# Heads paired with the next but one, joined loads of later batches and a reordered w_in, in a fused sliding-window attention and leaky-ReLU MLP kernel

## The chip, the cores and the metric

The kernel runs on one core of one Trainium2 chip. The metric is the time of one execution on the device in microseconds, taken as the median over several runs. A core has five engines that run on their own instruction streams, each in program order: TensorE (PE, with its weight loads shown as PEld), VectorE (DVE), ScalarE (ACT), GpSimd (POOL) and SyncE (SP). Here SP does nothing but issue transfers (DMAs), which sixteen DMA engines carry out.

## The reference

Attention with a mask for each head, then a two-layer MLP over all tokens:

```python
B, H, S, D = 8, 8, 576, 64           # q, k, v: (B, H, S, D), float32
scores = q @ k^T / sqrt(D)
rel = pos[:, None] - pos[None, :]
mask_plain = (rel >= 0) & (rel < 32)                        # heads 0 to 3
mask_dil = (rel >= 0) & (rel < 128) & (rel % 4 == 0)        # heads 4 to 7
attn = softmax(where(mask, scores, -1e9))
x = (attn @ v).transpose(0, 2, 1, 3).reshape(B * S, H * D)  # 4608 x 512
h = x @ w_in                                                # w_in: 512 x 2048
out = maximum(0.01 * h, h) @ w_out                          # w_out: 2048 x 512
```

## The kernel before

All of w_in and w_out is held in SBUF as 16-bit floats. The batches of attention are worked in order, and two batches make 1152 tokens of x^T in `xt`, with 128 of the 512 rows of x^T in each of four blocks. These are the outputs of a pair of heads, 64 rows for each. The MLP takes the tokens in chunks of 384: `up` (L983) makes hidden columns by four products over the four blocks of `xt` and the four 128-row parts of w_in, ScalarE applies the leaky ReLU into `gt`, and `down` and `group` multiply by w_out. `group` takes four tiles of 128 tokens at a time and saves one product in eight with sums of blocks.

Nothing of the order is left to the hardware. Every operation is a task with a cost in microseconds, a priority and dependencies. `_Plan.run` (L97) lays the tasks out on the engines in a planned time, and each engine's instructions are then issued in the order of those planned starts. So a planner's cost changes the order, never the work. A transfer's planned cost has an issue on SP (0.42 for all, in `load`, L265), a service on one server for all DMAs (`took`, L258) and a margin `LATE`. `WHEN` (L17) holds the planned start of each batch.

Four heads make a group. Within a batch the group of dilated heads comes first, then the plain one (`attend`: pairs 2, 3, 0, 1). A pair is two heads that stand side by side, 0 and 1, 2 and 3 and so on; one head has partitions 0 to 63, the other 64 to 127.

`load_group` (L350) loads a group. Batch 0 and 1 are "early" and loaded in a form of their own. For batches 2 to 7 q and k each come as eight transfers, for each pair `j` one for every 32 partitions `a`, of 18 runs of 32 numbers on each partition:

```python
lo = [[load("SP", at(st, 32 * a, 32 * a + 32, j * S, [32, 18], [1, 32]),
            dram(src, base + (2 * j + a // 2) * HS + (a % 2) * 32,
                 [D, 32], [32 * D, 18], [1, 32]),
            576, 128, s_old, prio) for a in range(4)] for j in range(2)]
```

They land in staging buffers `stg` (four of them for late groups, one for q or k of a group), are cast by POOL into `nat` (three buffers, one for a pair), turned by VectorE and POOL into `slots`, and multiplied on TensorE in `late_unit` (L902): scores, Exp on ScalarE, a mask multiply on VectorE (`ee`, L952), sums and values, and a division into `xt` (L971). Plain v of a late group comes in four transfers of 64 x 9 x 64 numbers, dilated v in six smaller ones. All loads go on SP's queue; a load waits for its staging buffer to be free, and holds up what stands behind it on SP.

`load_rest` (L453) loads the last 64 rows of q and k of the early batches as 8 heads x 16 x 256 numbers. `load_w` (L484) loads the weights, w_in in eight transfers of 128 rows x 1024 columns (0.5 MB each):

```python
src = dram(moe_w_in, n % 4 * 128 * DFF + x, [DFF, 128], [1, 1024])
```

Transfers 0 to 3 hold the first 1024 columns of the four row parts, and 4 to 7 the others. `FIRST` (L20) orders the loads of the start: in it `i` is a w_in transfer, `o` a w_out transfer, and the others are q, k and v of the first two batches. `store` (L1034) writes results from three output tiles `osb`, on SP's queue as well.

Of the kernel before, what the change touches and what calls it, by code (L numbers as in the profile page):

```python
# [12 lines left out]
ALU = mybir.AluOpType  # L13

WIN = 32
AHEAD, LATE = 5.0, 4.0
WHEN = (-5.0, 15.0, 50.0, 77.0, 112.0, 138.0, 172.0, 200.0)  # L17
CON = -1484.5
AFTER = -1495.0
# [38 lines left out]

class _Task:
    __slots__ = ("choices", "eng", "lat", "deps", "fn", "prio", "soft", "n", "start", "done",  # L60
                 "dur", "left", "ready", "users", "service", "kind", "late")

    def __init__(self, choices, lat, deps, fn, prio, soft, n, kind):
        self.choices, self.lat, self.fn = choices, lat, fn
        self.prio, self.soft, self.n, self.kind = prio, soft, n, kind
        self.deps = [d for d in deps if d is not None]
        self.eng = self.start = self.done = self.dur = None
        self.left = 0
        self.ready = 0.0
        self.users = []  # L70
        self.service = self.late = 0.0


class _Plan:
# [22 lines left out]
    def run(self):  # L97
        free, waiting = {}, {}
        server = 0.0

        def enter(t):
            for eng, _ in t.choices:
                waiting.setdefault(eng, []).append(t)

        for t in self.tasks:
            for d in t.deps:
                d.users.append(t)
            t.left = len(t.deps)
            if t.left == 0:
                enter(t)  # L110
        order = []
        while len(order) < len(self.tasks):
            best = None
            for eng, cand in waiting.items():
                if not cand:
                    continue
                here = free.get(eng, 0.0)
                if eng == "SP":
                    here = max(here, server - AHEAD)
                could = [t for t in cand  # L120
                         if not self.better_elsewhere(t, eng, max(here, t.ready), free)]
                if not could:
                    continue
                at = max(here, min(t.ready for t in could))
                pick = min(((t.ready + t.soft > at + 1e-9, t.prio, t.n), t)
                           for t in could if t.ready <= at + 1e-9)
                if best is None or (at, pick[1].n) < best[:2]:
                    best = (at, pick[1].n, eng, pick[1])
            at, _, eng, t = best
            for e, _ in t.choices:  # L130
                waiting[e].remove(t)
            t.eng, t.start, t.dur = eng, at, dict(t.choices)[eng]
            free[eng] = at + t.dur
            if t.service:
                begin = max(at + t.dur + 0.9, server)
                server = begin + t.service
                t.done = server + 1.1 + t.late
            else:
                t.done = at + t.dur + t.lat
            order.append(t)  # L140
            for u in t.users:
                u.ready = max(u.ready, t.done)
                u.left -= 1
                if u.left == 0:
                    enter(u)
        order.sort(key=lambda t: (t.start, t.n))
        return order
# [3 lines left out]
def kernel(  # L151
# [112 lines left out]

    def load(queue, dst, src, n, size, deps, prio, slow=1.0):  # L265
        eng = ENG[queue]
        return plan.dma(queue, 0.42, took(n, size) * slow, deps,
                        lambda e: eng.dma_start(dst, src), prio,  # L268
                        LATE if prio > -1500 + len(FIRST) else 0.8 if prio >= AFTER else 0.0)

# [79 lines left out]
    def load_group(b, g, prio, prio_v):  # L350
# [7 lines left out]
        for o, src in ((0, q), (1, k)):  # L358
            sn, s_old = stage_slot(early, s_users := [])
            st = stg[sn]  # L360
            if first:
                lo = [load("SP", at(st, 0, 128, j * 512, [256, 2], [1, 256]),
                           dram(src, base + 2 * j * HS, [4 * D, 128], [HS, 2], [1, 256]),
                           256, 1024, s_old, prio + 0.3 * j + 0.1 * o) for j in range(2)]
            elif early:
                lo = [load("SP", at(st, 0, 128, 0, [256, 4], [1, 256]),
                           dram(src, base, [4 * D, 128], [HS, 4], [1, 256]),
                           512, 1024, s_old, prio)]
            else:
                lo = [[load("SP", at(st, 32 * a, 32 * a + 32, j * S, [32, 18], [1, 32]),  # L370
                            dram(src, base + (2 * j + a // 2) * HS + (a % 2) * 32,
                                 [D, 32], [32 * D, 18], [1, 32]),
                            576, 128, s_old, prio) for a in range(4)] for j in range(2)]
            stage.append((st, s_users))
            loads.append(lo)

# [4 lines left out]
                       dram(v, base, [4 * D, 128], [HS, 4], [1, 256]), 512, 1024, v_old, prio_v)]  # L381
            v_late[b] = vs, v_old, v_users
        elif dil:
            lv = [[load("SP", at(vs, 64 * h, 64 * h + 64, j * S, [256, 2], [1, 256]),
                        dram(v, base + (2 * j + h) * HS, [4 * D, 64], [256 * D, 2], [1, 256]),
                        128, 1024, v_old, prio_v) for j in range(2)] + [
                   load("SP", at(vs, 64 * h, 64 * h + 64, 512, [S, 2], [1, D]),
                        dram(v, base + h * HS + 512 * D, [D, 64], [2 * HS, 2], [1, D]),
                        128, 256, v_old, prio_v)] for h in range(2)]
        elif early:  # L390
            lv = []
# [7 lines left out]
                                96, 256, v_old, prio_v), t_vz]  # L399
                lv.append(lj)  # L400
        else:
            lv = [[load("SP", at(vs, 64 * h, 64 * h + 64, j * S, [D, 9], [1, D]),
                        dram(v, base + (2 * j + h) * HS, [D, 64], [64 * D, 9], [1, D]),
                        576, 256, v_old, prio_v) for j in range(2)] for h in range(2)]

        if not early:
            kn, k_old = ring("VK", NK, k_users := [])
# [11 lines left out]
        for j in range(2):  # L419
            nn, n_old = ring("NAT", NNAT, n_users := [])  # L420
            na, c_qk = nat[nn], []
            for o in range(2):
                st, s_users = stage[o]
                if early:
                    dst = at(na, 0, 128, o * 512, [D, 2], [128, 4], [1, D])
                    src = at(st, 0, 128, j * 512, [256, 2], [D, 4], [1, D])
                    n = 512
                else:
                    dst, src, n = na[:, o * S:o * S + S], st[:, j * S:j * S + S], S
                c_qk.append(cast(dst, src, n, (loads[o][j:j + 1] if first else loads[o] if early else loads[o][j]) + n_old, prio,  # L430
                                 (("ACT",) if o else ("DVE",)) if first and dil and j == 0 else
                                 CENG if early else ("POOL",)))
                s_users.append(c_qk[-1])
            if not early:
# [3 lines left out]
            dn, d_old = ring("VD" if dil else "VP", NV, d_users := [])  # L438
            vt = (vd if dil else vp)[dn]
            n_v = 256 if dil else 384  # L440
            h_a, h_s = 2 * j * n_v, n_v
            n, w = n_v // D, 128 * (8 if dil else 6)
            c_v = [cast(at(vt, 0, 128, 0, [w, 2], [128, n], [1, D]),
                        at(vs, 0, 128, h_a, [h_s, 2], [D, n], [1, D]), 2 * n_v,
                        (lv if dil else lv[j]) + d_old, prio_v)]
            v_users += c_v
            seen_ones[b, 2 * g + j] = [t_ones["d" if dil else "p", dn]]
            kept[b, 2 * g + j] = vt, d_users
# [4 lines left out]
    def load_rest(b, prio):  # L453
# [18 lines left out]
        for vi in (2, 3, 0, 1):  # L472
            vt, d_users = kept[b, vi]
            c_v = []
            if vi >= 2:
                c_v = [cast(at(vt, 0, 64, 0, [1024, 2], [128, 4], [1, D]),
                            at(vs, 0, 64, 1024 + (vi - 2) * 512, [256, 2], [D, 4], [1, D]), 512,
                            [lv] + d_users, prio + 30)]
                v_users += c_v
            visits[b, vi, 1] = rest, [c], r_users, vt, c_v + seen_ones[b, vi], d_users  # L480
# [3 lines left out]
    def load_w(n, prio):  # L484
# [5 lines left out]
        old = w_used[prev] if prev is not None else []  # L490
        if n < 8:
            x = n // 4 * 1024
            src = dram(moe_w_in, n % 4 * 128 * DFF + x, [DFF, 128], [1, 1024])
            dst, x = w_in, n % 4 * DFF + x
        else:
            x = 1024 * (n - 8)
            src = dram(moe_w_out, 128 * x, [2 * DM, 128], [1, 1024])
            dst = w_out
# [85 lines left out]
    def turn(b, hp, part, prio):  # L584
# [90 lines left out]
        if part == 1:  # L675
# [9 lines left out]
                new = pair_moves[b, hp ^ 1]  # L685
            else:
                new, busy = [], users + other[1] * (two == 2)
                for hh, h in enumerate(heads_of(b, hp)):
                    p0 = 64 * hh
                    for o, bk in ((0, qb), (1, kb)):  # L690
                        x, dims = 512 * o + 16 * h, [[128, 4], [1, 16]]
                        if dil:
# [3 lines left out]
                        else:  # L696
                            c, to = hh * S + 488, [[24, 4], [1, 16]]
                        step = PAD + S if o else 2 * S
                        new.append(move(at(bk, p0, p0 + 64, c, [step, two], *to),
                                        at(tpb, p0, p0 + 64, x, [32, two], *dims), 64 * two,  # L700
                                        [tq] + zq + zk + (busy if dil and o else []), prio))
                pair_moves[b, hp] = new
            q_users += new
# [330 lines left out]
    def store(ob, i, c, tt, c0, n_o, t_c, users, both=False):  # L1034
        for n_p, (p0, tok, n, by) in enumerate(rows(c, tt)):
            users.append(load("ACT" if both and n_p else "SP",
                              dram(out, tok * DM + c0, [by * DM, n], [1, n_o]),
                              ob[p0:p0 + n, i:i + n_o], n, 4 * n_o, [t_c], -3000))

    def down(c, tt, acts, at_time):  # L1040

# [359 lines left out]
```

## Time and profile before

| | |
|---|---|
| median of 3 runs | 354.02 us (350.91 to 355.02) |
| profiled execution, its own time | 354.57 us |
| span of its instructions | 352.8 us |
| TensorE busy | 309.0 us (88%), 2838 matmuls |
| VectorE, ScalarE, GpSimd busy | 206.5, 192.3, 128.5 us |
| granted TensorE clock, mean | 0.966 |
| transfers issued on SP | 421 |
| moved by DMA | 47.64 MB, 135 GB/s in the mean |

The span is that of the instructions in the profile; the execution's own time has 1.8 us more around it. The page has the span in 40 equal slices, with a digit for the busy tenths of each engine, and a list of idle times with the engine, line and tile that ended them (an arrow `<-` is read "waited for"). A `q` behind an engine's name (SPq) stands for its instruction queue: time in which it issues a transfer or waits, rather than computes. L268 is the line in `load` where every transfer is issued, and L278 the line of the casts, so that only the tile's name tells which is meant.

### The profile page before, as it was taken

The numbers are of one execution on the slowest core, as the hardware profiler recorded it, in microseconds if no ns is written. First come the engines' busy times: TensorE is split into PE (matmuls) and PEld (weight loads), VectorE is DVE, ScalarE is ACT, GpSimd is POOL, SyncE is SP. The second block draws the span as 40 slices with busy tenths as digits, with TensorE's granted clock in tenths as the row PEclk, the third lists the DMA queues.
The fourth block names the chain that finished last, engine by engine and source line by source line (L and its number), as shares of the span: only waits on it lengthen the run. The fifth ranks groups of instructions, "written<-read, shape, count | busy, mean of one in ns | idle before, by whom it ended". The sixth has DMA issues, their size and how long they took to land.

```text
span 352.8 us, 7717 instructions
## 1 busy us (share of the span) xinstructions
PE 309.0 (88%) x2838; PEld 221.8 (63%) x2838; DVE 206.5 (59%) x407; ACT 192.3 (55%) x465; POOL 128.5 (36%) x179
## 2 busy tenths in 40 slices
PE   8788898998789698859785987995999999999996
PEld 3534554678666576637563765764778777777775
DVE  5736997769748488424845873966462444015161
ACT  4835855877656475524680644643565584544422
POOL 3468555794553473246324644515000000000000
PEclk9999999999999899969996998998999999999999
DMA  7999989588679964576677768457300301021133
GB/s 252 294 335 372 390 228 161 129 141 150 139 133 141 122 138 95 122 129 143 119 153 129 142 131 142 128 111 151 94 17 14 91 0 32 0 91 32 30 92 89
DMA packets 159030, 47.64 MB, mean 135 GB/s; under 512 B 139024, under 2 KB 156304, under 8 KB 158992
## 3 DMA queue, kind: packets, MB, share of 16 engines
q1 hardware_dynamic: 158416, 46.79, 58.3%
q8 instruction: 22, 0.36, 0.4%
q10 hardware_dynamic: 576, 0.35, 0.4%
q14 instruction: 16, 0.13, 0.1%
HBM read 37.68 MB, written 9.44 MB: 134 GB/s over the span
## 4 chain that ended last, share of the span: by engine, by line
PE 35%; SPq 25%; DMA 21%; POOL 7%; DVE 5%; issue 4%; ACT 1%; POOLq 0%; DVEq 0%
SPq L268 25%; PE hps L999 16%; PE fps L1142 11%; DMA stg<-in_k_dram 7%; DMA stg<-in_q_dram 6%; PE tp L1142 3%; DMA wst<-in_moe_w_out_dram 3%; POOL nat L278 3%; DMA wst<-in_moe_w_in_dram 3%; DMA vst<-in_v_dram 3%; PE ops L942 2%; POOL slots L629 1%; POOL v_all L278 1%; DVE ee L952 1%; PE ops L1142 1%
## 5 line engine op out<-in xcount | busy, mean ns | idle before, releaser
L999 PE MATMUL hps<-xt,w_in 128*128 128x384 f16 (+1 forms) x812 | 151.0, 319 | 1.9 <-DVE slots L282 0.8
L1010 ACT ACTIVATE gt<-hps 128x384 f16<-128x384 f32 (+1 forms) x203 | 94.0, 468 | 74.7 <-PE hps L999 73.5
L999 PEld LDWEIGHTS <-w_in 128*128 128x128 f16 x832 | 75.2, 99 | 36.9 <-issue 3.9
L1142 PEld LDWEIGHTS <-gt 128*128 128x128 f16 x768 | 74.3, 99 | 15.6 <-issue 1.0
L278 POOL CAST nat<-stg 128x576 f16<-128x576 f32 (+1 forms) x53 | 36.8, 696 | 60.5 <-DMA stg<-in_k_dram 35.0
L278 POOL CAST v_all<-vst 64x1152 f16<-64x1152 f32 (+3 forms) x36 | 37.3, 1040 | 37.4 <-DMA vst<-in_v_dram 33.6
L1142 PE MATMUL fps<-w_out,gt 128*128 128x256 f16 x368 | 49.0, 278 | 0.0
L608 DVE STREAM_TRANSPOSE slots<-nat 64x64 f16<-64x64 f16 (+1 forms) x48 | 24.2, 504 | 16.0 <-POOL nat L278 15.4
L971 DVE TENSOR_TENSOR xt<-ops,rc 128x288 f16<-128x288 f32 x48 | 26.5, 552 | 10.9 <-PE ops L942 6.0
L623 DVE STREAM_TRANSPOSE turned<-nat 128x576 f16<-128x576 f16 (+1 forms) x24 | 17.5, 737 | 23.2 <-POOL nat L278 21.6
L942 PEld LDWEIGHTS <-sides 128*128 128x128 f16 x240 | 14.1, 102 | 23.9 <-issue 22.2
L952 DVE TENSOR_TENSOR ee<-ee,late_m 128x384 f16<-128x384 f16 (+1 forms) x48 | 22.4, 486 | 10.9 <-ACT ee L949 10.8
L1179 DVE TENSOR_TENSOR osb<-tp,stg 128x512 f32<-128x512 f32 x14 | 9.6, 684 | 28.7 <-ACT stg L1171 18.0
L942 PEld LDWEIGHTS <-v_all 128*128 128x128 f16 x240 | 15.9, 102 | 14.8 <-issue 9.8
L942 PE MATMUL ops<-ee,v_all 128*128 128x96 f16 (+2 forms) x240 | 17.4, 206 | 8.7 <-DVE xt L971 7.7
L942 PE MATMUL sps<-ee,sides 128*128 128x96 f16 (+2 forms) x120 | 8.7, 207 | 17.5 <-DVE ee L952 17.5
L1171 ACT COPY stg<-fps 128x512 f32<-128x512 f32 (+1 forms) x27 | 14.5, 538 | 15.8 <-PE fps L1142 15.3
L960 ACT ACTIVATE rc<-sps 128x288 f32<-128x288 f32 x24 | 9.8, 410 | 20.9 <-PE sps L942 20.9
L963 ACT ACTIVATE rc<-rc 128x288 f32<-128x288 f32 x48 | 20.8, 446 | 0.2
L629 POOL COPY slots<-turned 64x512 f16<-64x512 f16 x24 | 17.1, 713 | 4.1 <-DVE turned L623 3.3
L570 DVE COPY slots<-tp 64x128 f16<-64x128 f16 (+7 forms) x43 | 13.6, 334 | 7.1 <-PE tp L649 6.6
L642 DVE STREAM_TRANSPOSE slots<-nat 128x576 f16<-128x576 f16 x12 | 9.3, 775 | 14.2 <-POOL nat L278 14.0
(113 smaller groups left out, 420.7 us busy)
## 6 DMA issues: line engine op xcount, KB each, us to landing
stg<-in_q_dram SPq DMA_DIRECT2D x96, 72.0 KB, 2.3
stg<-in_k_dram SPq DMA_DIRECT2D x96, 72.0 KB, 2.3
vst<-in_v_dram SPq DMA_DIRECT2D x24, 144.0 KB, 3.3
vst<-in_v_dram SPq DMA_DIRECT2D x24, 128.0 KB, 2.8
gt<-in_moe_w_in_dram SPq DMA_DIRECT2D x5, 512.0 KB, 8.2
xt<-in_moe_w_out_dram SPq DMA_DIRECT2D x3, 512.0 KB, 10.7
gt<-in_moe_w_out_dram SPq DMA_DIRECT2D x3, 512.0 KB, 10.2
out_dram<-osb SPq DMA_DIRECT2D x12, 128.0 KB, 2.1
```

Of the source, the lines that this page charges most:

```text
L268: lambda e: eng.dma_start(dst, src), prio,
L278: ENG[e].tensor_copy(out=dst, in_=src)
L608: nc.vector.transpose(at(qb, p0, p0 + 64, p0 + c, *dims), na[p0:p0 + 64, S + c // 2:S + c // 2 + n])
L623: lambda e, xb=xb, o=o, n=n: nc.vector.transpose(xb[:, 0:n], na[:, o * S:o * S + n]),
L629: lambda e, xb=xb, p0=64 * h: ENG[e].tensor_copy(out=at(qb, p0, p0 + 64, p0, [128, 4], [512, 2], [1, 64]), in_=at(xb, p0, p0 + 64, 0, [1, ...
L942: nc.tensor.matmul(at(bk, 0, 128, o, *dims), stationary(s), et[:, c:c + n], start=i == 0, stop=i == len(parts) - 1, skip_group_check=True)
L952: lambda e: nc.vector.tensor_tensor(out=et[:, 0:w], in0=et[:, 0:w], in1=mk, op=ALU.mult), prio + 0.1)
L963: lambda e: nc.scalar.activation(out=rt[:, 0:NQ], in_=rt[:, 0:NQ], func=AF.Exp, scale=-1.0),
L971: lambda e: nc.vector.tensor_tensor(out=dst, in0=at(ot, 0, 128, 0, *src), in1=at(rt, 0, 128, 0, *src), op=ALU.mult), prio + 0.2)
L999: nc.tensor.matmul(ht[:, 0:n], at(w_in, 0, 128, i * DFF + j // 2 * 256 + j % 2, [2, 128]), at(xt[m % 2], 0, 128, i * 1152 + x0 + x, [1, n] ...
L1010: lambda e: nc.scalar.activation(out=gt[c % NG][:, j * n_c + x:j * n_c + x + n], in_=ht[:, 0:n], func=AF.Prelu, alpha=0.01),
L1142: nc.tensor.matmul(bk[:, x:x + HN], tl[:, off + j * step:off + j * step + 128], rhs(j), start=first and x == 0 and j == 0, stop=j == HJ - ...
```

## The change

- A pair is now head `i` and head `i + 2` of its group: (0, 2), (1, 3), (4, 6), (5, 7). For each staging partition the rows of its two pairs then lie one behind the other in memory, so that later q and k come in four transfers of 36 runs on each of 32 partitions, in place of eight of 18, and later plain v in two of 18 in place of four of 9. Later dilated v stays at six transfers, cut otherwise. Casts and moves follow with other head strides; the cast of a pair now waits for the loads of both.
- Rows of x^T so change places between blocks, and w_in is loaded with its rows in the same order: each 128-row transfer takes two blocks of 64 rows that lie 128 rows apart.
- The planner counts an issue of the joined loads with 0.66 or 0.95 us and others with 0.45, and takes the result of an output tile as ready for its stores 5 us later than it is (`HOLD`), except in the last group. In the instruction streams made from it, SP has 313 transfers, and TensorE 2839 matmuls (one idle filler more).

```diff
-AHEAD, LATE = 5.0, 4.0
+AHEAD, LATE, HOLD = 5.0, 4.0, 5.0
...
-                u.ready = max(u.ready, t.done)
+                u.ready = max(u.ready, t.done + u.hold)
...
-        return plan.dma(queue, 0.42, took(n, size) * slow, deps,
+        return plan.dma(queue, {1152 * 128: 0.66, 1152 * 256: 0.95}.get(n * size, 0.45), took(n, size) * slow, deps,
...
             if first:
...
-                           dram(src, base + 2 * j * HS, [4 * D, 128], [HS, 2], [1, 256]),
+                           dram(src, base + j * HS, [4 * D, 128], [2 * HS, 2], [1, 256]),
...
             else:
-                lo = [[load("SP", at(st, 32 * a, 32 * a + 32, j * S, [32, 18], [1, 32]),
-                            dram(src, base + (2 * j + a // 2) * HS + (a % 2) * 32,
-                                 [D, 32], [32 * D, 18], [1, 32]),
-                            576, 128, s_old, prio) for a in range(4)] for j in range(2)]
+                lo = [load("SP", at(st, 32 * a, 32 * a + 32, 0, [32, 36], [1, 32]),
+                           dram(src, base + (a // 2) * 2 * HS + (a % 2) * 32,
+                                [D, 32], [32 * D, 36], [1, 32]),
+                           1152, 128, s_old, prio) for a in range(4)]
...
         else:
-            lv = [[load("SP", at(vs, 64 * h, 64 * h + 64, j * S, [D, 9], [1, D]),
-                        dram(v, base + (2 * j + h) * HS, [D, 64], [64 * D, 9], [1, D]),
-                        576, 256, v_old, prio_v) for j in range(2)] for h in range(2)]
+            lv = [[load("SP", at(vs, 64 * h, 64 * h + 64, 0, [D, 18], [1, D]),
+                        dram(v, base + 2 * h * HS, [D, 64], [64 * D, 18], [1, D]),
+                        1152, 256, v_old, prio_v)] for h in range(2)]
...
-            src = dram(moe_w_in, n % 4 * 128 * DFF + x, [DFF, 128], [1, 1024])
+            src = dram(moe_w_in, (n % 4 // 2 * 256 + n % 2 * 64) * DFF + x, [128 * DFF, 2], [DFF, 64], [1, 1024])
...
+            users[-1].hold = 0.0 if both else HOLD
```

More of the change, by code (lines that the diff above doesn't have):

```diff
@@ L60 @@
     __slots__ = ("choices", "eng", "lat", "deps", "fn", "prio", "soft", "n", "start", "done",
-                 "dur", "left", "ready", "users", "service", "kind", "late")
+                 "dur", "left", "ready", "users", "service", "kind", "late", "hold")
     def __init__(self, choices, lat, deps, fn, prio, soft, n, kind):
@@ L70, in __init__ @@
         self.users = []
-        self.service = self.late = 0.0
+        self.service = self.late = self.hold = 0.0
 class _Plan:
@@ L383, in load_group @@
         elif dil:
-            lv = [[load("SP", at(vs, 64 * h, 64 * h + 64, j * S, [256, 2], [1, 256]),
-                        dram(v, base + (2 * j + h) * HS, [4 * D, 64], [256 * D, 2], [1, 256]),
-                        128, 1024, v_old, prio_v) for j in range(2)] + [
+            lv = [[load("SP", at(vs, 64 * h, 64 * h + 64, 256 * i, [S, 2], [1, 256]),
+                        dram(v, base + 2 * h * HS + 256 * i * D, [4 * D, 64], [HS, 2], [1, 256]),
+                        128, 1024, v_old, prio_v) for i in range(2)] + [
                    load("SP", at(vs, 64 * h, 64 * h + 64, 512, [S, 2], [1, D]),
-                        dram(v, base + h * HS + 512 * D, [D, 64], [2 * HS, 2], [1, D]),
+                        dram(v, base + 2 * h * HS + 512 * D, [D, 64], [HS, 2], [1, D]),
                         128, 256, v_old, prio_v)] for h in range(2)]
@@ L425, in load_group @@
                     dst = at(na, 0, 128, o * 512, [D, 2], [128, 4], [1, D])
-                    src = at(st, 0, 128, j * 512, [256, 2], [D, 4], [1, D])
+                    src = at(st, 0, 128, *((j * 512, [256, 2]) if first else (j * 256, [512, 2])), [D, 4], [1, D])
                     n = 512
@@ L429, in load_group @@
                     dst, src, n = na[:, o * S:o * S + S], st[:, j * S:j * S + S], S
-                c_qk.append(cast(dst, src, n, (loads[o][j:j + 1] if first else loads[o] if early else loads[o][j]) + n_old, prio,
+                c_qk.append(cast(dst, src, n, (loads[o][j:j + 1] if first else loads[o]) + n_old, prio,
                                  (("ACT",) if o else ("DVE",)) if first and dil and j == 0 else
@@ L440, in load_group @@
             n_v = 256 if dil else 384
-            h_a, h_s = 2 * j * n_v, n_v
+            h_a, h_s = j * n_v, 2 * n_v
             n, w = n_v // D, 128 * (8 if dil else 6)
@@ L444, in load_group @@
                         at(vs, 0, 128, h_a, [h_s, 2], [D, n], [1, D]), 2 * n_v,
-                        (lv if dil else lv[j]) + d_old, prio_v)]
+                        (lv if dil else lv[0] + lv[1]) + d_old, prio_v)]
             v_users += c_v
@@ L476, in load_rest @@
                 c_v = [cast(at(vt, 0, 64, 0, [1024, 2], [128, 4], [1, D]),
-                            at(vs, 0, 64, 1024 + (vi - 2) * 512, [256, 2], [D, 4], [1, D]), 512,
+                            at(vs, 0, 64, 1024 + (vi - 2) * 256, [512, 2], [D, 4], [1, D]), 512,
                             [lv] + d_users, prio + 30)]
@@ L687, in turn @@
                 new, busy = [], users + other[1] * (two == 2)
-                for hh, h in enumerate(heads_of(b, hp)):
-                    p0 = 64 * hh
+                for hh in range(2):
+                    h, p0 = 4 * (hp // 2) + hp % 2 + 2 * hh, 64 * hh
                     for o, bk in ((0, qb), (1, kb)):
@@ L699, in turn @@
                         new.append(move(at(bk, p0, p0 + 64, c, [step, two], *to),
-                                        at(tpb, p0, p0 + 64, x, [32, two], *dims), 64 * two,
+                                        at(tpb, p0, p0 + 64, x, [16, two], *dims), 64 * two,
                                         [tq] + zq + zk + (busy if dil and o else []), prio))
```

## The prediction

> **What bounds the kernel now.** I read the page's slices first, then the busy time by stretch, the queue's own waits, TensorE's waits with its timeline, the chain of waits, the list of DMA issues, and last the trace's single records of packets and landings. The slices:
>
> ```profile
> PE   8788898998789698859785987995999999999996
> ...
> PEclk9999999999999899969996998998999999999999
> DMA  7999989588679964576677768457300301021133
> ```
>
> There are three stages. Up to about 55 us the 16 DMA engines are full; from there to about 245 TensorE has holes and its clock dips; after that TensorE is full. The stretches (columns: busy time of each engine, granted clock, share of the DMA engines, GB/s) put sizes to it:
>
> ```profile
> 20.00:40.00 20.00, 16.94 (x134) 9.62 (x132) 11.57 (x34) 11.31 (x26) 14.62 (x24) 1.00 1.06 364
> ...
> 140.00:160.00 20.00, 14.31 (x117) 10.37 (x116) 9.08 (x18) 7.97 (x19) 6.64 (x9) 0.83 0.64 126
> ...
> 180.00:200.00 20.00, 15.03 (x130) 10.51 (x128) 11.09 (x21) 7.70 (x21) 8.44 (x10) 0.83 0.68 133
> ```
>
> From 60 to 260 us TensorE's busy times add up to 169.5, so it is idle for 30.5 us, and the shortfall of the clock in the same rows is worth another 12 at most. TensorE's waits and its timeline name the holes:
>
> ```profile
> PE sps L942 <- DVE ee L952: 17.5, 7, 5.7
> PE ops L942 <- DVE xt L971: 7.7, 7, 5.0
> ```
> ```profile
> 154.32 0.50 PE L942 MATMUL sps<-ee,sides 128*128 128x96 f16 x5 [5.69 <-DVE ee L952]
> ```
>
> VectorE is named, but it too was waiting. Through the same hole the chain of waits runs over the SP queue, a landing and POOL's cast:
>
> ```profile
> 149.68 0.50 SPq L268
> 150.22 2.17 DMA stg<-in_q_dram
> 152.54 0.67 POOL nat L278
> ```
>
> VectorE's order has transposes of the next group ahead of the mask that TensorE waits for, and those wait for q and k. The supply of q, k and v, thus SP's queue, bounds the middle stage: SP issues from 50.6 to 243.5 us almost without a pause. The first stage is bounded by the weights and the first loads; its chain has this piece:
>
> ```profile
> 13.68 9.61 DMA wst<-in_moe_w_in_dram
> ```
>
> **The change, part by part.**
>
> *w_in rows (eight loads of 512 KB, all in the first 30 us).* The source was 128 rows in a row; it is now written 2 x 64 x 1024, the destination 128 x 1 x 1024, and the program carries both so. Nothing in the trace of before has a source with a slowest count of 2. The nearest rows are the leftover loads of `load_rest`: source 8 x 16 x 256, destination 128 x 1 x 256. In the trace's record of landings each of the four leaves 9 marks on its semaphore, and every other transfer leaves 16 (54 issues give 857, 850 and 857 marks on the three semaphores concerned, which is 864 less 7 for each leftover load). In each the first mark comes early and alone (15.58 us, for a load issued at 14.41), and eight follow with the data (21.60 to 22.41). I read that as eight engines in place of sixteen, one per outer source block, and take two engines for an outer count of 2. The other ends are eight engines (any split source) and sixteen (no effect).
>
> [...]
>
> The price: a packet of 4096 bytes takes 0.160 us in the packet records (least 0.156, median 0.164). On sixteen engines a load is 8 packets on each, 1.28 us; on two it is 64, 10.24 us. All eight loads fall on the same two engines, one after the other. The last load ahead of them was issued at 10.12 and landed 5.17 later, at 15.3. So the eighth lands at 15.3 + 8 x 10.24 + 1.7 (the leftover loads between them: 36 packets of 1024 bytes at 0.046) = 98.9. Before, it landed here:
>
> ```profile
> xt<-in_moe_w_in_dram SPq DMA_DIRECT2D x1, 512.0 KB, 7.3
> ```
>
> Issued at 21.44, it landed at 28.7. The shift is 70 us (68 by the least packet; 79 by the mean packet of 0.177, which holds the crowding of sixteen full engines). What could hide it? Transfers behind it on the queue use the same two engines too, so w_out, batch 1 and the mask table come behind: before, these took from 28.7 to 55.2, with the engines full, and they take as long again. TensorE runs in order; its first w_in product stood at 18.4 us, the first one that needs the second half of w_in at 26.4. By 98.9 it can have done only the 18 us of streaming that stand before that. I hide nothing: the whole rest moves by 70. With eight engines it would be 8 x 1.28 = 10; with sixteen, nothing.
>
> *Later q and k (192 transfers of 576 runs of 128 bytes become 96 of 1152).*
>
> ```profile
> stg<-in_q_dram SPq DMA_DIRECT2D x96, 72.0 KB, 2.3
> ```
>
> SP's time from one such issue to the next is 0.54 us (median) and 0.59 (mean, with pauses of about 1 us every 20 issues or so): 192 x 0.59 = 113 us. The upper end after is no gain, 96 x 1.18 = 113, if the issue goes with the runs. Against that, 128 runs on 64 partitions cost 0.60 us and 576 runs 0.64, so SP's own cost hardly depends on them; SP alone would fall to some 96 x 0.6 = 58. But the DMA engines set a floor: a packet of 128 bytes takes 12.5 ns, 72 of them on each engine 0.90, with the mark 0.92; 96 x 0.92 = 88. I take 88: saved 25. The first pair of a group now waits for 4 x 0.92 in place of 4 x 0.54, 1.5 us more; the second pair, no longer than before. This lies within the two groups that the staging buffers hold ahead.
>
> [...]
>
> *Later plain v (24 become 12).* Mean 0.74 each, 18 us. After: 72 packets of 256 bytes at 18.5 ns, 1.33 each, 16: saved 2. Dilated v (36 issues, 28 us) keeps its count. The 62 stores that stand among the loads (32 us) stay 62.
>
> *Stores held 5 us in the plan.* In the middle stage SP waits 0.4 us on an output tile, so that is all there is to gain. Three output tiles turn over some 7 us apart (a tile's second product), so a buffer has 21 us for a store of about 2 us of issues and 2 of landing; 5 more fit. If they did not, the eviction would wait and TensorE behind it; now that wait is 0.3 us.
>
> *Order and addresses.* Casts, moves and matmuls keep their counts and lengths, only head strides change. In TensorE's order the units of batches 2 to 4 stand up to 2.7 us of work later, the others within 2 of where they stood; three idle fillers more. Batch 0's plain values wait for both loads, which land by 15.3, ahead of w_in. Together 0, within 3 either way.
>
> *Sum.* SP's middle stage: 193 - 25 - 2 = 166 us, so the last loads come 27 us sooner after their start. Stalls that end on these loads go with them, and the lost 30.5 + 12 holds that much: -27 (nothing to -42). Next late is TensorE itself. Profiled execution 354.6 (span 352.8 and 1.8 around it), which is 0.6 above the median of the runs: 354.6 + 70 - 27 = 398. Where a store follows joined loads, SP issues it while the engines still hold packets. Twelve runs of stores stand among the loads; at half a store's issue each, some 0.25 us, that takes 3 more off: **395**. A floor: after 98.9 TensorE has about 269 us of streaming left (matmuls at full clock) and some 8 of tail gaps: 378 with the 1.8.
>
> **The rivals.**
>
> *w_in still uses sixteen or eight engines* (not slower). For it: no row shows two. Against: 9 marks in four of four cases. The point that decides is whether the last w_in load lands near 29 (or 39) or near 99. Then only the savings stand: 354.6 - 30 = 325, or 335 with eight. Chance 0.09, faster.
>
> *Four engines*, the landing at about 59: 8 x 5.12 less 10.24, +31, and it cancels: 355. Chance 0.02.
>
> *Two engines, and the joined loads save little*, SP taking about 1.1 for each as its issue goes with the runs: 354.6 + 70 - 6 = 419. For it: the median 0.50 of these issues against 0.43 for stores of few runs. Against: 0.60 to 0.64 above. Chance 0.12.
>
> *Two engines, and the middle stage loses nearly all its holes*: 380, near the floor. For it: the DMA share is only 0.64 and 0.68 in the stretches above. Against: 0.92 x 4 before each first pair. Chance 0.15.
>
> **How the numbers follow.** The forecast, two engines with 24 to 36 us won back, has 0.62: 395, by itself 388 to 403. The three cases with two engines hold 0.89; the range 377 to 420 takes in the low rival and about half of the high one. Differences of 1% are about what a measurement of this kernel can tell, as its own runs lie 350.9 to 355.0. Slower 0.89, within 1% 0.02, faster 0.09.
>
> **What would show it.** In the list of DMA issues, w_in takes tens of us to land, and a DMA share under 0.3 stands in the slices between 20 and 95 us with TensorE idle; the first w_in products stretch to about 100; late q begins near 120. Then q and k land 0.9 us apart, and the holes of 5 us and the half-speed clock of the middle stage are gone or short. A w_in landing near 29 us would make the first term wrong; q and k still 1.1 apart, the second.

## The result, and the profile after

The changed kernel takes 407.97 us (median of 4 runs, 404.93 to 410.13), the kernel before 354.48 in the same comparison: a ratio of 1.153, 95% interval 1.142 to 1.164. The forecast was 395 in a range of 377 to 420. The profiled execution of after took 410.13 us, its span is 408.3, its mean granted clock 0.883. Here and below, ratios leave out runs of more than 1.5% above the fastest of the same kernel, while medians and ranges keep them.

The slices of the page after:

```profile
PE   6631341110988999898969796898879999999996
...
PEclk9955556555799999999979999899989999999999
DMA  8411211136979898999948997999651020002032
```

A slice is 10.2 us. From the third to the ninth, some 20 to 92 us, the DMA engines have a busy share of one to three tenths, TensorE one of one to four tenths, and its clock stands near half. The stretches (columns as before: busy time of PE, PEld, DVE, ACT and POOL, granted clock, DMA share, GB/s):

```profile
20.00:40.00 20.00, 4.85 (x17) 1.65 (x16) 2.31 (x7) 0.69 (x2) 2.21 (x3) 0.52 0.13 52
...
80.00:100.00 20.00, 2.08 (x12) 0.99 (x10) 0.00 (x0) 0.98 (x2) 1.17 (x2) 0.50 0.43 136
...
140.00:160.00 20.00, 18.95 (x235) 15.72 (x234) 16.32 (x28) 16.40 (x48) 15.94 (x21) 1.00 1.12 153
...
180.00:200.00 20.00, 18.02 (x203) 13.86 (x201) 13.38 (x27) 13.91 (x34) 11.00 (x15) 1.00 1.28 142
200.00:220.00 20.00, 16.52 (x146) 12.28 (x143) 12.17 (x21) 8.94 (x22) 6.53 (x7) 0.83 0.79 121
```

From 20 to 40 us 52 GB/s flow where 364 did, and 0.13 of sixteen engines is two engines: 2/16 = 0.125. From 120 us on the stage that was full of holes is denser. Its busy times from 120 to 320 us add up to 178.7, so TensorE idles for 21.3 us, against 30.5 before in 60 to 260. The waits of TensorE (in total, times, the longest):

```profile
PE hps L999 <- POOL w_in L278: 35.0, 4, 10.3
PE hps L999 <- DVE w_in L278: 14.9, 2, 8.1
PE ops L942 <- DVE xt L971: 12.1, 9, 3.4
...
PE sps L942 <- DVE ee L952: 5.8, 3, 3.5
```

The first two are new: products of `up` that wait for a cast of w_in, in steps of up to 10.3 us, the time between two landings. The mask wait fell from 17.5 us to 5.8, and the wait for x^T rose from 7.7 to 12.1. The longest hole that is left in the middle stage:

```profile
209.70 0.48 PE L942 MATMUL sps<-ee,sides 128*128 128x96 f16 x5 [3.48 <-DVE ee L952]
```

In the chain of waits (start, length, what) the kernel hangs first on one issue, then on the last w_in load:

```profile
53.80 10.13 SPq L268
63.98 36.76 DMA xt<-in_moe_w_in_dram
```

SP is held 10.13 us in one issue, as long as a w_in load takes; the eighth w_in load is issued behind it and lands at 100.7, 11.6 us after the seventh. The list of issues gives no time for such a load, since it leaves too few marks to be matched:

```profile
stg<-in_q_dram SPq DMA_DIRECT2D x48, 144.0 KB, 4.7
...
gt<-in_moe_w_in_dram SPq DMA_DIRECT2D x5, 512.0 KB
```

The trace's single records have them: three marks a load, two with the data and one at once, at 25.29, 35.37, 45.49, 55.65, 68.02, 78.11, 89.09 and 100.73 us. Between 30 and 90 us there are 2.0 packets of 4096 bytes in flight, each 0.161 us.

Where the 55.5 us between the two profiled executions went: the first load of late q is issued at 120.9 in place of 50.6 (+70.3), the first late unit's scores start at 140.8 in place of 69.0 (+71.8), the last unit at 339.3 in place of 283.7 (+55.6), and the end is later by 55.5. So 72 were lost before the middle stage, it won back 16, and the tail did nothing.

### The profile page after: what moved, and what is told of

The parts are those of the page before. It is cut to its first block, busy times and chain, and to the rows that moved or that the text cites. A ratio compares the mean times of both kernels' runs of the same rounds, so it can differ in the third digit from the quotient of the medians.

```text
span 408.3 us, 7547 instructions
## 1 busy us (share of the span) xinstructions
PE 313.1 (77%) x2839; PEld 223.8 (55%) x2839; DVE 203.7 (50%) x408; ACT 191.8 (47%) x464; POOL 128.2 (31%) x179
## 4 chain that ended last, share of the span: by engine, by line
PE 38%; SPq 26%; DMA 19%; DVE 6%; POOL 5%; issue 4%; ACT 1%; POOLq 0%; DVEq 0%
SPq L268 26%; PE hps L999 16%; PE fps L1143 10%; DMA xt<-in_moe_w_in_dram 9%; DMA stg<-in_q_dram 5%; DMA stg<-in_k_dram 4%; PE tp L1143 4%; PE fps L1052 3%; POOL nat L278 2%; DVE gt L1129 2%; POOL slots L629 1%; DVE xt L971 1%; PE ops L942 1%; PE ops L1143 1%; DVE slots L608 1%
## 5 line engine op out<-in xcount | busy, mean ns | idle before, releaser
L999 PE MATMUL hps<-xt,w_in 128*128 128x384 f16 (+1 forms) x812 | 152.8, 322 | 56.7 <-POOL w_in L278 35.0
L999 PEld LDWEIGHTS <-w_in 128*128 128x128 f16 x832 | 76.5, 101 | 95.3 <-POOL w_in L278 36.5
L1143 PEld LDWEIGHTS <-gt 128*128 128x128 f16 x768 | 75.6, 100 | 17.6 <-DVE gt L1129 1.3
L1143 PE MATMUL fps<-w_out,gt 128*128 128x256 f16 x368 | 48.0, 274 | 0.0
L278 POOL CAST v_all<-vst 64x1152 f16<-64x1152 f32 (+3 forms) x36 | 38.4, 1075 | 20.0 <-DMA vst<-in_v_dram 19.1
L608 DVE STREAM_TRANSPOSE slots<-nat 64x64 f16<-64x64 f16 (+1 forms) x48 | 24.0, 500 | 11.6 <-POOL nat L278 11.1
L952 DVE TENSOR_TENSOR ee<-ee,late_m 128x384 f16<-128x384 f16 (+1 forms) x48 | 23.8, 515 | 10.8 <-ACT ee L949 10.5
L817 ACT ACTIVATE ee<-sps 128x384 f16<-128x384 f32 x20 | 9.8, 490 | 36.6 <-PE sps L795 29.2
L942 PE MATMUL ops<-ee,v_all 128*128 128x96 f16 (+2 forms) x240 | 16.9, 203 | 12.3 <-DVE xt L971 12.1
L623 DVE STREAM_TRANSPOSE turned<-nat 128x576 f16<-128x576 f16 (+1 forms) x24 | 17.7, 739 | 10.2 <-POOL nat L278 8.4
L278 DVE CAST nat<-stg 128x512 f16<-128x512 f32 x10 | 4.6, 460 | 32.7 <-DMA stg<-in_q_dram 31.8
L278 POOL CAST w_in<-gt 128x512 f16<-128x512 f32 x8 | 5.2, 676 | 44.8 <-DMA gt<-in_moe_w_in_dram 44.8
L1143 PE MATMUL fps<-wst,gt 128*128 128x256 f16 x128 | 19.0, 300 | 0.0
## 6 DMA issues: line engine op xcount, KB each, us to landing
gt<-in_moe_w_out_dram SPq DMA_DIRECT2D x3, 512.0 KB, 10.1
```

Source lines behind the costliest of these rows:

```text
L278: ENG[e].tensor_copy(out=dst, in_=src)
L608: nc.vector.transpose(at(qb, p0, p0 + 64, p0 + c, *dims), na[p0:p0 + 64, S + c // 2:S + c // 2 + n])
L623: lambda e, xb=xb, o=o, n=n: nc.vector.transpose(xb[:, 0:n], na[:, o * S:o * S + n]),
L942: nc.tensor.matmul(at(bk, 0, 128, o, *dims), stationary(s), et[:, c:c + n], start=i == 0, stop=i == len(parts) - 1, skip_group_check=True)
L952: lambda e: nc.vector.tensor_tensor(out=et[:, 0:w], in0=et[:, 0:w], in1=mk, op=ALU.mult), prio + 0.1)
L999: nc.tensor.matmul(ht[:, 0:n], at(w_in, 0, 128, i * DFF + j // 2 * 256 + j % 2, [2, 128]), at(xt[m % 2], 0, 128, i * 1152 + x0 + x, [1, n] ...
```

## The experiments

My theory was that of the prediction: the outermost count of the w_in source is the number of DMA engines that carry it. The rivals were that something else in the change costs the time, and, for what is won back, that it does not come from the joined loads. All times stand beside the kernel before in the same comparison, whose medians are 354.2 to 355.4 us. In e1, e3, e4, e6, e7, e8 and e11 the rows of w_in are not those of x^T: the work is the same, but the output is not the reference's.

**w_in read as before (e1).**

```diff
-src = dram(moe_w_in, (n % 4 // 2 * 256 + n % 2 * 64) * DFF + x, [128 * DFF, 2], [DFF, 64], [1, 1024])
+src = dram(moe_w_in, n % 4 * 128 * DFF + x, [DFF, 128], [1, 1024])
```

> The changed kernel, but w_in is read as 128 rows in a row again; the rows then do not match those of x^T, so the output is not the reference's. Theory (w_in on two engines costs some 72 us, the rest of the change gives back some 16): 410 - 72 = 338 us, first late load issued near 50 us, sixteen marks for each w_in load. Rival (the new pairing, the joined loads or the new order on the engines make it slow, w_in costs little): 395 us or more.

Measured: 337.34 us (335.07 to 337.82), ratio 0.950 (0.945 to 0.955). The last w_in load lands at 27.96, late q starts at 50.8. One line of the change costs 407.97 - 337.34 = 70.6 us; the rest of it gains 18.0.

**The change to w_in alone, in the kernel before (e3).** The same line, the other way.

> The kernel before with nothing but the changed source of w_in (2 x 64 rows); the rows do not match x^T, so the output is not the reference's. Theory: 354.5 + 71 = 425 us, as nothing of the middle stage is won; three marks for each w_in load. Rival (the two parts of the change make it slow only together): 354 to 370 us.

Measured: 426.75 us in 2 runs, ratio 1.203 (1.195 to 1.212), so +71.4. Its slices:

```profile
PEclk9965555555999999998997897998989999999999
DMA  8411111149967776696466767766572011002032
```

The empty stretch is that of after; behind it stand the half-filled slices of the kernel before (mostly 6 and 7 tenths), which in after mostly read 7 to 9.

**Four blocks, and eight (e4, e11).** Source `[128 * DFF, 4], [DFF, 32], [1, 1024]`, and `[64 * DFF, 8], [DFF, 16], [1, 1024]`.

> The changed kernel with w_in read as 4 blocks of 32 rows, 128 rows apart, in each load (other rows than x^T has, so the output is not the reference's). Theory (engines as many as outer blocks): five marks a load, 32 packets an engine, 5.1 us a load, +31 us against sixteen engines: 338 + 31 = 369 us. Rival (any source in blocks is slow, by its addresses): 400 us or more, as with two blocks.

> After, with the w_in source as eight blocks of 16 rows (64 rows apart, so other rows than x^T's; this part of the output differs), only for the dose. By the theory that the outermost count of the source is the number of engines: nine landing marks a load, 16 packets of 0.160 us in series on each of eight engines, 2.56 us a load at the least; eight loads take 10 us more than on sixteen engines: 345 to 350 us (e1 is 337, e4 with four blocks 370). If it were not the count: 337 or 370 and more.

Measured: 370.49 and 348.76 us, one run each. The landing marks are five and nine a load, the packets of 4096 bytes stay at 0.161 and 0.165 us, and the last w_in load lands at 61.9 and 42.4. TensorE's waits, with four blocks and with eight:

```profile
PE hps L999 <- POOL w_in L278: 16.7, 4, 5.1
```
```profile
PE hps L999 <- POOL w_in L278: 9.3, 4, 3.3
```

The wait shrinks with the interval between landings: 10.3, 5.1 and 3.3 us at the longest. With 2, 4, 8 and 128 for the outermost count, which I read as 2, 4, 8 and 16 engines, the kernel takes 408.0, 370.5, 348.8 and 337.3: +70.6, +33.2, +11.4 and 0, where the prediction's series said +70, +31 and +10. The marks 3, 5 and 9 are one more than the count each time; a w_in load of 128 rows leaves 16 in the kernel before. The DMA share agrees: from 15 to 45 us 18 of the 20 slices of 1.5 us read 2 tenths with four blocks (4/16 = 0.25), and from 15 to 27 us all eight read 4 or 5 with eight (8/16 = 0.5).

**Each w_in load as two halves (e2).** Each 64-row block by itself, so that its outermost count is 64; the casts wait for both.

```diff
-t = load("SP", st, src, 128, 4096, old, prio, 1.3 if n < 4 else 1.0)
+ts = [load("SP", st[64 * s:64 * s + 64], src[s], 64, 4096, old, prio, 1.3 if n < 4 else 1.0)
+      for s in range(2)]
```

> The changed kernel with the same rows of w_in, each load cut into two transfers of 64 partitions with 64 rows in a row each. Theory: each half has a slowest count of 64 and goes to sixteen engines, so 338 us, up to 342 if the eight more issues at the start cost their 0.4 us each. Rival (the reordered rows of w_in are slow to read, in whatever transfer): some 400 us.

Measured: 347.26 us (346.13 to 348.43), ratio 0.980 (0.973 to 0.986): some 2% faster than before, but 9.9 us over the kernel with the old rows, and I had expected at most 5. The stretches, first with the old rows, then with the halves:

```profile
20.00:30.00 10.00, 8.13 (x57) 4.34 (x56) 3.94 (x17) 3.72 (x10) 8.96 (x15) 1.00 1.06 350
30.00:40.00 10.00, 9.32 (x86) 5.82 (x83) 8.48 (x21) 8.51 (x20) 5.89 (x10) 1.00 1.06 380
```
```profile
20.00:30.00 10.00, 8.35 (x43) 3.92 (x42) 3.37 (x13) 3.35 (x10) 4.49 (x7) 0.86 1.05 212
30.00:40.00 10.00, 4.57 (x26) 2.45 (x27) 2.00 (x8) 1.50 (x4) 5.49 (x11) 0.65 1.06 246
```

The share of the DMA engines is the same, 1.05 and 1.06, but the bytes fall from 350 and 380 GB/s to 212 and 246. By that share all sixteen engines work, each at about half its rate: a packet of 4096 bytes takes 0.299 us here (median from 16 to 35 us) against 0.162 with the old rows. So a half of 64 partitions takes about as long as a whole load of 128, the last half lands at 39.2, and late q starts at 59.7 in place of 50.8. Why the packets take 1.8 times as long, no run shows: that all sixteen engines then write to one half of the partitions was my theory in e5. The rival, that the rows or the size of the halves are slow, can be read in the same trace: of the first 32 packets of the first half, 24 take under 0.2 us (median 0.159), and of the 64 packets that follow the first 64 none does (0.298). Packets of the same size and of like rows thus start at full speed and slow down only as the flow lasts. A short transfer doesn't show it: dilated v goes to 64 partitions too, 128 KB at a time, and in the kernel before its packets of 1024 bytes take 0.046 us in the median, against 0.047 for those to 128 partitions in the first 12 us.

**The second half on GpSimd's queue (e5)**, to let both halves flow at once (the planner counts 1.0 us for an issue there):

```diff
-ts = [load("SP", ...
+ts = [load(("SP", "POOL")[s], ...
```

> As e2 (each w_in load in two halves of 64 partitions), but the second half is issued by GpSimd on its own queue, so that halves for both partition halves are under way at once. In e2 the packets of 4096 bytes took 0.299 us in place of 0.160. Theory A (a destination of 64 partitions takes only half the rate, as all sixteen engines write to one half of the partitions): packets come near 0.16 to 0.20 again and the time comes down to 338 to 342 us, unless the halves on GpSimd, which overtake the first q, k and v, put off batch 0 by up to 6 us. Theory B (the halves are slow by their source rows or their size): packets stay near 0.30 and the time at 347.

Measured: 349.19 us in 2 runs, ratio 0.988 (0.980 to 0.995). It doesn't decide between the theories, because the halves never met. GpSimd issued five of its eight halves from 3.6 to 6.0 us, ahead of the first q, k and v; SP's came behind those: none of their packets before 25 us, when GpSimd's were through. The packets take about 0.26 to 0.33 us on both queues, each queue in its own time, so total and time are those of the halves on one queue.

**The rows moved by the casts (e9, and e10 with VectorE).** If only the load is narrow, w_in can be read as before, and the casts from 32 to 16 bits put the rows in order:

```diff
+for s in range(2):
+    y = (n % 4 // 2 * 2 + s) * DFF + x + 512 * i
+    h = n % 2 * 64
+    c = cast(w_in[h:h + 64, y:y + 512], st[64 * s:64 * s + 64, 512 * i:512 * i + 512], 512, [t],
...
```

> As after, but w_in is read as before, in blocks of 128 consecutive rows by all sixteen engines, and its rows are put in the new order by the casts: a load brings two heads' 64 rows, and each half is cast by itself, to partitions 0-63 or 64-127 of the chunk to which it belongs; 32 casts of 64 partitions x 512 in place of 16 of 128 partitions x 512. The whole computation is kept. Theory A (only the engines of the w_in load were wrong with the change, and 64 partitions are half as wide only for a DMA): the w_in loads land as in e1, the last near 28 us; 16 more casts of about 0.65 us are 10 us more of GpSimd, which is busy 35 of the first 60 us in e1, so that most of it lies beside other work: late q from 50 to 56 us, 338 to 344 us. Theory B (GpSimd bounds the first 40 us: it is busy 9 of the 10 us from 20 to 30 in e1): the extra 10 us stand ahead of the q, k casts, staging buffers come free late, and the time is 346 to 350.

> As e9, but VectorE may take the casts of the last four w_in loads too, which only GpSimd did. Theory A: within 2 us of e9. Theory B: 3 to 8 us under e9.

Measured: 336.54 us (333.4 to 338.9), ratio 0.944 (0.938 to 0.949), and 335.62 (334.85 to 337.39), ratio 0.948 (0.944 to 0.952). Like the halves, these two keep the whole computation and beat both kernels, and by more; they don't differ from each other. Of the first, the groups of casts from one of the three staging tiles (count, busy time and mean ns, idle time before), and the stretches:

```profile
L278 POOL CAST w_in<-gt 64x512 f16<-64x512 f32 x16 | 10.1, 631 | 1.4 <-DMA gt<-in_moe_w_in_dram 0.7
L278 DVE CAST w_in<-gt 64x512 f16<-64x512 f32 x4 | 2.8, 706 | 1.3 <-DMA gt<-in_moe_w_in_dram 1.2
```
```profile
20.00:30.00 10.00, 7.51 (x49) 4.04 (x49) 6.83 (x21) 3.66 (x9) 8.76 (x15) 1.00 1.06 341
30.00:40.00 10.00, 6.56 (x58) 3.59 (x57) 8.63 (x17) 4.33 (x9) 9.36 (x14) 1.00 1.05 388
```

A cast of 64 partitions takes 631 ns on GpSimd, in the mean of those that stay in their half and those that change it; one of 128 took 663 with the old rows. Half as wide takes 5% less, and there are twice as many: over all staging tiles 20.6 us of casts on GpSimd and VectorE in place of 9.9. GpSimd is busy 18.1 of these 20 us (14.9 with the old rows) and TensorE does 3.4 us less here. But the loads keep their 341 and 388 GB/s, the last w_in lands at 29.7, and late q starts at 50.6, which is what the end follows.

**What is won back: the joined loads (e6), the hold (e7), the costs (e8).** From the kernel with the old rows I took one of these away at a time: q, k and plain v in 18 and 9 runs again (the pairs and the rest as in the change), the hold, the new costs.

```diff
-lo = [load("SP", at(st, 32 * a, 32 * a + 32, 0, [32, 36], [1, 32]),
+lo = [[load("SP", at(st, 32 * a, 32 * a + 32, j * S, [32, 18], [1, 32]),
...
-AHEAD, LATE, HOLD = 5.0, 4.0, 5.0
+AHEAD, LATE, HOLD = 5.0, 4.0, 0.0
...
-return plan.dma(queue, {1152 * 128: 0.66, 1152 * 256: 0.95}.get(n * size, 0.45), took(n, size) * slow, deps,
+return plan.dma(queue, 0.42, took(n, size) * slow, deps,
```

> As e1 (w_in as before, rows that do not match x^T), but later q and k again in eight transfers of 576 runs and plain v in four, for the new pairs; planner's costs and the hold stay. Theory (the joined loads shorten SP's middle stage and give the 18 us): SP's stage back to some 190 us from 172, time 352 to 357 us. Rival (the new costs and the hold make the better order): 338 to 344 us.

> As e1, with the hold of stores at 0. Theory (stores among the loads now stand behind full rings and cost SP 39.7 us in place of 33.1; a hold of 5 us in the plan changes little of that): 335 to 341 us. Rival (the hold keeps SP from waiting on output tiles and is a part of the gain): 343 us or more, with waits of SP on osb in the middle stage.

> As e1, with the planner's old cost of 0.42 us for every issue. Theory (the plan's loads are bound by its one server, not by the issue, so the order hardly changes): 335 to 341 us. Rival (the truer costs are what places the transposes rightly): 343 us or more.

Measured: without the joins 351.41 us (349.13 to 354.05 in 10 runs), ratio 0.993 (0.989 to 0.997); without the hold 337.62, ratio 0.955 (0.950 to 0.959); with the old cost 340.30 in 2 runs. Against 337.34, the joins are worth 14.1 of the 18.0 us, the hold nothing, the costs about 3. The first is just under its expected 352 to 357: what the change still has without the joins (pairs, order, costs and hold) gives some 3 us. SP's time from the first late load to the end of the last is 193 us again, from 172.5.

**Stores on ScalarE's queue (e12)**, in the kernel whose casts move the rows, to see what the stores cost SP:

```diff
-users.append(load("ACT" if both and n_p else "SP",
+users.append(load("SP" if both and not n_p else "ACT",
```

> As e9 (all of the computation kept), with the 62 stores that stand among the later loads issued by ScalarE's queue; SP then only loads. In e9 SP's late stage is 174 us: 94 of q and k, 39 of stores, 41 of v. Theory A (the joined loads keep the DMA engines themselves full, their share is 0.95 from 60 to 240 us in e9, and a store on SP only waits for room that the loads behind it would wait for too): q and k come no closer together, the time that stores took on SP goes to longer issues of the loads, SP's late stage stays over 160 us, and the time is within 4 us of e9, 333 to 341, with ScalarE's 62 issues of about 0.5 us as a cost. Theory B (SP's own time bounds the stage, and each store costs it 0.6 us): the stage is 135 to 150 us, TensorE's holes of the middle (some 18 us from 60 to 240) go, 320 to 331 us.

Measured: 379.45 to 386.45 us in 4 runs, 43 to 50 over e9; both theories missed. The timeline of ScalarE shows why:

```profile
136.31 10.15 ACTq L268 DMA_DIRECT2D out_dram<-osb  x18
146.50 0.87 ACT L1015 ACTIVATE gt<-hps 128x384 f16<-128x384 f32 x2 [9.77 <-DMA out_dram<-osb]
```

Eighteen issues in a row hold ScalarE for 10.15 us, the next leaky ReLU comes 9.77 us late, and TensorE's products of `up` wait behind it. SP, which now loads and does little else, waits too (from 50 to 260 us: in total, times, the longest):

```profile
SPq L268 <- DMA out_dram<-osb: 65.0, 16, 11.9
```

No buffer is behind these waits. In the records the transfers of SP and ScalarE take eight landing semaphores in turn. The twelve longest of these waits, 64 of the 65 us, each end within 0.03 us of the landing of a store that had the same semaphore: the longest ends at 141.09, when a store has landed that ScalarE issued at 138.09, among the eighteen. I read from this that the issue waited for the transfer that had its semaphore before. So the loads on SP still hung on the stores, now through ScalarE's order. The price of a store on SP stays open by this run, since the new stalls cover it.

## Why the prediction came out right

- **w_in on two engines, +70: right.** Three marks a load; 100.73 where 98.9 was forecast; +70.3 at the issue of late q; 70.6 and 71.4 us by the two experiments on this line alone. That nothing hides it held too. The prediction weighed one row, the leftover loads with nine marks, which it took for one engine per outer block; the series of 2, 4 and 8 blocks agrees with this reading.
- **The rivals with sixteen, eight or four engines** fell with the marks. Their prices for 4 and 8 blocks, +31 and +10, were measured as +33 and +11.
- **The middle stage, -30: the direction right, the size too large.** It gave 16 back in after, 18.0 without the w_in line. The time from the first late load to the end of the last was 193 us before and 175 after, where 166 was forecast. So the median of 407.97 lies above the 388 to 403 that the forecast gave its own case, about as far from 395 as from the 419 of the rival in which the joins save little; the range of 377 to 420 holds it. That the joins are nevertheless what gains is shown by the run without them. The parts of the stage, as the sums of SP's times from one issue to the next:

| | before | after | change | forecast |
|---|---|---|---|---|
| later q, k | 113.7 | 92.3 | -21.4 | -25 |
| plain v | 17.8 | 13.2 | -4.6 | -2 |
| dilated v | 28.3 | 31.4 | +3.1 | 0 |
| 62 stores | 33.1 | 38.3 | +5.2 | -3 |

- **The mis-sized term is the stores,** 8.2 of the 12 us by which these parts fall short. The prediction said that SP issues a store "while the engines still hold packets", at a gain of 3 us. But a store's time on SP rises from 0.53 to 0.62 us in the mean, and dilated v's with it. In e1 a store takes 0.64 and dilated v 29.2 us, so the most of it does not come from w_in; in e6, which is e1 without the joins, they take 0.52 and 25.8, so it comes with the joins. What SP saves on fewer issues it partly spends on the others. Fuller engines are the likely reason: from 60 to 240 us their share is 0.96 in e1 and 0.69 in e6. But the bytes are 143 and 133 GB/s, and the records of 128-byte packets are longer (17.5 ns in the mean, 12.8 in e6), so most of that difference is longer records, not more flow. That full engines hold up these issues is read from these rows, not tested alone, and the full rings in e7's expectation were an assumption that no run shows.
- **q and k "0.92 each" by the floor of packets: right within 5%**, 0.96 in the mean and 0.87 in the median. Plain v went under its floor, 1.09 us each in place of 1.33, so the time of the packets is no bound for a pair of issues. All the joins together were worth 14.1 us (e6 against e1), and the 1.1 us each of the rival in which the joins save little did not come.
- **Holes:** forecast gone or short. The longest of the middle stage fell from 5.69 to 3.48 us, and half-speed clock is granted there in three places where there were five. That is the other side of the 14 us missing: idle time fell from 30.5 to 21.3, not to nothing.
- **Hold and order, 0 within 3: right** (0.3 us, and about 3 at its edge). TensorE has one idle filler more, not three.

The forecast was worked out for the profiled execution. Against its 410.13 us some 15 are missing: these 14 of the middle stage, and not quite 2 of the first, behind which the late units' scores start 71.8 us later in place of 70. The median lies 2 us under that execution.

## What to carry to other kernels

Before a load's source is rewritten, look at its outermost count: w_in loads of 0.5 MB that landed 1.28 us apart (24.86, 26.14 and 27.42 us in the kernel before) landed 10.1 us apart and more because 128 rows became 2 x 64, and no count of bytes or transfers shows that, only the marks and the packets in flight. If rows have to change places, do it where an instruction handles them anyway: here casts by half the partitions cost 10.7 us of two side engines and nothing of the time, while splitting the load cost 10 us of it. When transfers on a queue are joined, ask what else is issued there: here the stores took 5.2 us more of SP and dilated v 3.1, a third of what the joins saved it. And before transfers move to another queue, look at what they go on sharing: eight landing semaphores tied SP's loads to ScalarE's order, for 64 us of waits in e12.

## What the runs showed of the hardware

Loads of 256 KB to 64 partitions, one behind the other, used all sixteen engines and yet ran at half rate: packets of 4096 bytes took 0.299 us against 0.162 for 128 partitions, so a busy share of 1.05 carried 212 GB/s in one kernel and 1.06 carried 350 in another. A high DMA share here said that the engines were occupied, not that bytes flowed at full rate. A cast of half the partitions saved 5% of its time: 631 ns on GpSimd for 64, 663 for 128.
